# Attention, soft MoE and a squared-ReLU layer on one core: w_in converted by quarters, scores in two PSUM banks

## The chip, the cores and the metric

The kernel runs on one core of a Trainium2 chip. Times are device microseconds (us) of one execution; the kernel before took 434.12 us in the median of three runs (428.06, 434.12, 439.13). Five engines matter: PE (TensorE, matrix products into PSUM), DVE (VectorE), ACT (ScalarE), POOL (GpSimd), and the DMA queues, nearly all of whose transfers are issued by SP. Each engine takes its instructions in the order in which the program lists them; across engines they wait on semaphores.

## The reference

```python
# B=4 batches, H=8 heads, 512 local + 32 global tokens, head size 64, all float32
out_g = softmax(q_g k_all^T / 8) v_all           # 32 global tokens see all 544 keys
out_l = softmax([q_l k_g^T, band(q_l k_l^T)] / 8) [v_g, v_l]   # band: |i - j| <= 32
x = concat(out_g, out_l) -> (2176, 512)
logits = x @ phi                                 # phi (512, 32): 8 experts of 4 slots
slot_in = softmax_over_tokens(logits).T @ x      # (32, 512)
slot_out[e] = relu(slot_in[e] @ w1[e]) @ w2[e]   # w1 (8,512,1024), w2 (8,1024,512)
x = softmax_over_slots(logits) @ slot_out        # (2176, 512)
h = relu(x @ w_in)                               # w_in (512, 2048), float64 in memory
return (h * h) @ w_out                           # w_out (2048, 512), float64 in memory
```

## The kernel before, in words

Everything is written out in order by hand (no scheduler moves it), and lies in four stages.

**Attention, 0 to 169 us.** There are 44 units: 32 local ones (16 blocks of 32 queries, times two halves of the heads) and 12 global ones. Unit n goes through S (scores, `emit_S`, PE, L330 local and L336 global), mask and row minimum on DVE (L341, four instructions, from PSUM into `s_buf`), a subtraction on POOL (L354), the exponential on ACT (L364), T (four transposes on PE, L372, into the PSUM tile `pp`, copied out by ACT or DVE), and AV (products with V, L391). The loop is a software pipeline: iteration n lists S of unit n, the exponential of n-1, AV of an earlier pair, T of n-2. In between lie the transposes of new keys and queries (L219), of finished tokens (L212) and MoE logits (L442). S of a unit is 16 small products (2 head pairs, 4 batches, 2 heads e of a pair), each of which the profile records as two matmuls. A local product uses 64 of the 128 rows of the array (the half that head e owns) and 32 columns; the pair (batch, e) picks one of the four column quarters, so e=0 and e=1 never share a quarter, and all 16 write one PSUM bank, `sp`, of which there are two. A global product uses all 128 rows, with queries padded with zeros (`qgz`), and batch picks the quarter.

w_in and w_out are float64 and are turned into float32 on the chip, in blocks of 128 x 512 values (512 KB raw): `convert` is ACT abs (L540), DVE clamp and shift (L543, L546), the low word's rest (L551 on ACT or L553 on DVE), DVE join (L556), POOL add (L558). The first half of w_in, eight blocks, is converted during attention through one raw buffer `cv_raw`, at the units in the table `CONV`. The expert weights w1 and w2 are 64 pieces of 512 KB; `PIECES` says how many of them SP issues after each unit. 24 granules of SBUF ("room" a and b) can hold them at first, and more as buffers die.

**Soft MoE, 169 to 208 us.** The expert layers (`layer1` L916, `layer2` L944) use the pieces in order and free their room for the rest.

**Squared-ReLU layer, 208 to 433 us.** x @ w_in is computed as c @ G, with G = slot_out @ w_in (rank 32): `G_part`/`G_late` make G for some columns (PE, `gps`, L1023; one column quarter of the array for each 256 columns of G), `G_split` and `replicate` bring it into `G4`. There are 17 token tiles in three groups (6, 6, 5) and 16 chunks m of the 2048 hidden columns. One step (group, m) is `emit_h` (PE `hp` L1085; ACT relu L1088; DVE product L1089; then a high and low part, ACT L1095 and DVE L1096) and, one step later, `emit_o` (three 512-column matmuls per tile, L1140 to L1142, into one PSUM bank per tile). Iteration n lists h of step n, o of step n-1, then the conversion work planned for n. The order of steps is `passes`: group 0 with m 0 to 7, group 1 with m 0 to 15, group 0 with m 8 to 15, group 2 with all. At the end of a pass the tiles are copied out, or added to a saved sum (L1147, DVE). Here the remaining 8 blocks of w_in and 16 chunks of w_out are converted, one per step, over steps 0 to 23; a w_out chunk also needs `part`, ACT L859 and POOL L860, just before its first use.

Of the kernel before, what the change touches and what calls it, by code (L numbers as in the profile page):

```python
# [18 lines left out]
BIG = 3.0e38  # L19
# [5 lines left out]
def local_global_attention__soft_moe__relu2_kernel(  # L25
# [83 lines left out]
    win_sb = A.carve(NC, FF // 2)  # L109
# [6 lines left out]
    qgz = Bq.carve(HP, B, 2, QB)  # L116
# [6 lines left out]
    s_buf = Bq.carve(4, 128)  # L123
# [53 lines left out]
    def consts():  # L177
        zz = qgz.rearrange("p h b e q -> p (h b) e q")
        nc.vector.memset(zz[64:128, :, 0, :], 0.0)
        nc.vector.memset(zz[0:64, :, 1, :], 0.0)  # L180
# [49 lines left out]
    def global_q(qg_sb):  # L230
        tp = transpose4(qg_sb, ps_m, "m")
        for e in range(2):
            s = slice(64 * e, 64 * e + 64)
            evac(qgz.rearrange("p h b e q -> p (h b) e q")[s, :, e, :],
                 tp[s].rearrange("p h (b q) -> p (h b) q", b=B), e)
# [36 lines left out]
    for s in range(NJ):  # L272
# [29 lines left out]
    CONV = (4, 9, 13, 18, 22, 27, 31, 36)  # L302
    CONV_AT = (
        (0, 0, 1, 2, 3), (-1, 1, 1, 2, 3), (0, 0, 1, 2, 3), (0, 0, 0, 2, 3), (0, 1, 1, 2, 3), (0, 0, 0, 2, 3),
        (0, 1, 2, 2, 3), (0, 0, 1, 1, 2),
    )
    REST_ON_ACT = (0, 0, 1, 0, 1, 1, 1, 1)
# [5 lines left out]
        0, 0, 0, 0, 1, 2, 0, 0, 1, 1, 1, 1, 0, 1, 1, 1, 0, 0, 2, 2, 1, 0, 1, 1, 0, 1, 2, 1, 0, 1, 0, 0,  # L313
        3, 1, 0, 1, 1, 0, 1, 0, 4, 2, 2, 1,
    )

    def emit_S(n):
        kind, s, half = units[n]
        x0, s1, s2 = window(s)
        sp = ps_s.tile([128, 4, 128], F32, tag="s", name="sp")  # L320
        for h in range(2):
            hp = 2 * half + h
            for b in range(B):
                if kind == "l":
# [15 lines left out]
        for j in range(4):  # L340
            nc.vector.tensor_tensor_reduce(out=s_buf[:, j], in0=sp[:, j], in1=mk, scale=-scale, scalar=BIG,  # L341
# [12 lines left out]
        nc.gpsimd.tensor_tensor(out=pe.rearrange("p j (r k) -> p j k r", k=4), in0=s_buf.rearrange("p j (k r) -> p j k r", k=4),  # L354
# [852 lines left out]
```

## Time and profile before

| | |
|---|---|
| median of three runs | 434.12 us (428.06 to 439.13) |
| the profiled execution, whole / its span | 435.36 us / 433.5 us |
| busy share of the span: PE, DVE, ACT, POOL | 92%, 66%, 55%, 31% |
| mean granted PE clock | 0.988 of full speed |
| chain that ended last: PE, DVE, DMA, ACT | 57%, 15%, 12%, 8% |

Busy shares are means over stages with different limits; the windows and the chain of waits by stage tell more. A matmul's busy time includes its latency and overlaps its neighbours', so the pace of a run of matmuls is read from its length over its count.

### The profile page before, as it was taken

How to read it: one execution, taken by the hardware profiler on the slowest of the kernel's cores; microseconds unless marked ns; L12 is line 12 of the kernel's file. 1: busy time of each engine (PE TensorE's matmuls, PEld its weight loads, DVE VectorE, ACT ScalarE, POOL GpSimd, SP SyncE). 2: the span in 40 equal slices, each digit the busy share in tenths (PEclk: the TensorE clock that was granted, in tenths of full speed). 3: DMA queues.
4: the chain of work that ended last, by engine and by line, in shares of the span. 5: the costliest groups of instructions: out<-in, count | busy, mean ns of one | idle time of the engine just before them, and what ended most of it. 6: DMA issues, size and time to landing. Idle time of an engine off the chain costs nothing.

```text
span 433.5 us, 12427 instructions
## 1 busy us (share of the span) xinstructions
PE 400.9 (92%) x4897; PEld 306.5 (71%) x4897; DVE 287.6 (66%) x930; ACT 239.9 (55%) x561; POOL 134.4 (31%) x159
## 2 busy tenths in 40 slices
PE   6789869968889987999999999999999999999996
PEld 6677758756567764355567777777887888888884
DVE  5596947766567966310689999777997535744443
ACT  2678756878578443121656666565764534344442
POOL 6245524535346441110345532224553000000000
PEclk9999988999899999999999999999999999999999
DMA  5788894899375399899933334210000500410003
GB/s 145 193 250 220 267 279 127 284 284 305 105 222 196 88 375 356 318 409 406 406 126 98 100 103 139 97 50 0 2 0 21 121 6 0 106 42 2 0 1 121
DMA packets 54890, 69.02 MB, mean 159 GB/s; under 512 B 23856, under 2 KB 40496, under 8 KB 54832
## 3 DMA queue, kind: packets, MB, share of 16 engines
q1 hardware_dynamic: 53360, 67.19, 48.2%
q10 hardware_dynamic: 1472, 1.05, 0.8%
q8 instruction: 38, 0.62, 0.6%
q14 instruction: 20, 0.16, 0.1%
HBM read 63.77 MB, written 4.46 MB: 157 GB/s over the span
## 4 chain that ended last, share of the span: by engine, by line
PE 57%; DVE 15%; DMA 12%; ACT 8%; issue 5%; POOL 1%; SPq 1%; POOLq 0%; DVEq 0%; ACTq 0%
PE ops L1140 9%; PE ops L1141 9%; PE ops L1142 9%; PE sp L330 5%; PE xp L391 4%; PE pp L372 4%; ACT arena_b L146 4%; DVE arena_a L543 3%; DMA arena_b<-in_moe_w_in_dram 3%; DVE al L1096 3%; PE tp L219 3%; PE hps L916 2%; DMA arena_b<-in_moe_w_dram 2%; DMA arena_a<-in_moe_w_dram 2%; DVE arena_a L556 2%
## 5 line engine op out<-in xcount | busy, mean ns | idle before, releaser
L1140 PE MATMUL ops<-w_hl,ah 128*128 128x512 f32 x271 | 107.2, 395 | 0.0
L1141 PE MATMUL ops<-w_hl,ah 128*128 128x512 f32 x271 | 106.6, 393 | 0.6 <-POOL w_hl L860 0.6
L1142 PE MATMUL ops<-w_hl,al 128*128 128x512 f32 x271 | 105.7, 390 | 0.0
L1089 DVE TENSOR_TENSOR arena_a<-hp,arena_a 128x384 f32<-128x384 f32 x96 | 46.8, 529 | 45.4 <-ACT arena_a L1088 45.3
L1088 ACT ACTIVATE arena_a<-hp 128x384 f32<-128x384 f32 x96 | 40.2, 471 | 61.7 <-PE hp L1085 61.4
L1095 ACT ACTIVATE ah<-arena_a 128x384 fp32r<-128x384 f32 x96 | 45.0, 506 | 28.3 <-DVE arena_a L1089 28.3
L354 POOL TENSOR_TENSOR arena_r<-arena_b,nm 128x512 f32<-128x512 f32 x32 | 39.8, 1243 | 62.7 <-DVE nm L341 34.8
L1141 PEld LDWEIGHTS ops<-w_hl,ah 128*128 128x128 f32 x271 | 50.9, 188 | 11.6 <-POOL w_hl L860 2.8
L1142 PEld LDWEIGHTS ops<-w_hl,al 128*128 128x128 f32 x271 | 50.9, 188 | 11.1 <-DVE al L1096 0.2
L1140 PEld LDWEIGHTS ops<-w_hl,ah 128*128 128x128 f32 x271 | 50.9, 188 | 11.0 <-issue 0.8
L1096 DVE TENSOR_TENSOR al<-arena_a,ah 128x384 fp32r<-128x384 f32 x96 | 50.8, 569 | 8.9 <-ACT ah L1095 5.0
L146 ACT ACTIVATE arena_b<-tp 64x256 f32<-64x256 f32 (+2 forms) x151 | 48.8, 350 | 10.9 <-PE tp L219 5.7
L558 POOL TENSOR_TENSOR arena_a<-arena_a 128x512 int32<-128x512 int32 x23 | 29.8, 1296 | 53.1 <-DVE arena_a L556 46.2
L341 DVE CUSTOM_DVE_ANT_0 arena_b<-sp,arena_r 128x128 f32<-128x128 f32 x128 | 29.5, 286 | 20.4 <-PE sp L330 14.9
L330 PE MATMUL sp<-arena_b 64*32 64x128 f32 x1024 | 37.3, 281 | 4.0 <-issue 2.3
L330 PEld LDWEIGHTS sp<-arena_b 64*32 64x32 f32 x1024 | 27.4, 110 | 12.2 <-issue 9.7
L372 PE MATMUL pp<-ident,arena_r 128*128 128x128 f32 x176 | 29.5, 292 | 4.9 <-ACT arena_r L364 4.9
L391 PE MATMUL xp<-arena_v,arena_t 128*32 128x65 f32 x1408 | 27.2, 227 | 7.1 <-DMA arena_v<-in_v_l_dram 3.1
L364 ACT ACTIVATE arena_r<-arena_r 128x512 f32<-128x512 f32 x44 | 27.7, 629 | 9.7 <-POOL arena_r L354 9.4
L391 PEld LDWEIGHTS xp<-arena_v,arena_t 128*32 128x32 f32 x1408 | 22.7, 113 | 12.5 <-issue 6.6
L372 PEld LDWEIGHTS pp<-ident,arena_r 128*128 128x128 f32 x176 | 19.2, 144 | 12.3 <-ACT arena_r L364 6.4
L860 POOL TENSOR_TENSOR w_hl<-arena_a,w_hl 128x512 fp32r<-128x512 f32 x16 | 21.1, 1320 | 15.1 <-ACT w_hl L859 15.1
(194 smaller groups left out, 583.0 us busy)
## 6 DMA issues: line engine op xcount, KB each, us to landing
arena_a<-in_moe_w_dram SPq DMA_DIRECT2D x34, 512.0 KB, 6.1
arena_b<-in_moe_w_dram SPq DMA_DIRECT2D x23, 512.0 KB, 6.9
arena_a<-in_moe_w_out_dram SPq DMA_DIRECT2D x16, 512.0 KB, 5.3
arena_v<-in_v_l_dram SPq DMA_DIRECT2D x16, 256.0 KB, 4.4
arena_b<-in_moe_w_in_dram SPq DMA_DIRECT2D x8, 512.0 KB, 5.1
arena_a<-in_moe_w_in_dram SPq DMA_DIRECT2D x8, 512.0 KB, 3.9
arena_k<-in_k_l_dram SPq DMA_DIRECT2D x30, 128.0 KB, 4.1
arena_q<-in_q_l_dram SPq DMA_DIRECT2D x30, 128.0 KB, 3.6
```

Source lines behind the costliest of these rows:

```text
L146: nc.scalar.activation(out=out, in_=in_, func=AF.Copy)
L330: nc.tensor.matmul(sp[r + 32 * e:r + 32 * e + 32, j], qz[d, (s + 2) % 3, hp, b], keys, start=True, stop=True, tile_position=(64 * e, r + 3 ...
L354: nc.gpsimd.tensor_tensor(out=pe.rearrange("p j (r k) -> p j k r", k=4), in0=s_buf.rearrange("p j (k r) -> p j k r", k=4), in1=nm.unsqueez ...
L372: nc.tensor.transpose(pp[:, j], pe_buf[n % NPE][:, j], ident)
L391: nc.tensor.matmul(xp[32 * b:32 * b + 32, 2 * h + e], p, V[:, b, 4 * half + 2 * h + e], start=True, stop=True)
L1088: nc.scalar.activation(out=r[:, :N], in_=hp[:, :N], func=AF.Relu)
L1089: nc.vector.tensor_tensor(out=a[:, :N], in0=hp[:, :N], in1=r[:, :N], op=ALU.mult)
L1095: nc.scalar.activation(out=ah[:, s], in_=a, func=AF.Copy)
L1096: nc.vector.tensor_tensor(out=al[:, s], in0=a, in1=ah[:, s].bitcast(F32), op=ALU.subtract)
L1140: nc.tensor.matmul(op, ah[:, s], w_hi, start=begin, stop=False)
L1141: nc.tensor.matmul(op, ah[:, s], w_lo, start=False, stop=False)
L1142: nc.tensor.matmul(op, al[:, s], w_hi, start=False, stop=end)
```

## The change

1. **Quarters of w_in.** `CONV` has four blocks instead of eight; `win_sb` is half as large. Two more granules are free for weight pieces (13 in room a, 5 in a new room c, 8 in b), and `PIECES` issues some pieces earlier.
2. **Two groups take turns.** `passes` becomes group 0 with m 0 to 3, group 1 with 0 to 7, group 0 with 4 to 11, group 1 with 8 to 15, group 0 with 12 to 15, group 2 with all. 28 blocks are converted in this stage, over steps 0 to 27; their rest is always on ACT. G is made in four quarters; `G_late` runs three times, two steps before its first use, after the first tile of the step.
3. **Scores.** Each unit's scores go to two PSUM tiles, one per head e of a pair, out of three that go round; batch picks the column quarter and e the row half, for global units too (`qg` without padding). `s_buf` is doubled. To make room, `pp` has one PSUM buffer instead of two.

```diff
-    win_sb = A.carve(NC, FF // 2)
+    CW = 512
+    win_sb = A.carve(NC, CW)
...
+    s_buf = [Bq.carve(4, 128)]
...
-    room = {"a": A.granules(7, 23), "b": Bq.granules(10, 18), "t": []}
+    room = {"e": [], "a": A.granules(10, 23), "b": Bq.granules(10, 18), "c": A.granules(5, 10), "t": []}
...
-    ps_s = ps_att.enter_context(tc.tile_pool(name="ps_s", bufs=2, space=PSUM))
-    ps_pt = ps_att.enter_context(tc.tile_pool(name="ps_pt", bufs=2, space=PSUM))
+    ps_s = ps_att.enter_context(tc.tile_pool(name="ps_s", bufs=1, space=PSUM))
+    ps_pt = ps_att.enter_context(tc.tile_pool(name="ps_pt", bufs=1, space=PSUM))
...
-    CONV = (4, 9, 13, 18, 22, 27, 31, 36)
+    CONV = (4, 9, 13, 18)
...
-        0, 0, 0, 0, 1, 2, 0, 0, 1, 1, 1, 1, 0, 1, 1, 1, 0, 0, 2, 2, 1, 0, 1, 1, 0, 1, 2, 1, 0, 1, 0, 0,
+        0, 0, 0, 0, 1, 2, 0, 0, 1, 1, 1, 1, 0, 1, 1, 1, 0, 0, 2, 2, 1, 1, 1, 1, 0, 2, 2, 1, 0, 1, 1, 0,
...
+        q = qg if kind == "g" else qz[:, (s + 2) % 3]
+        sp = [ps_s.tile([128, 2, 128], F32, tag=f"s{(2 * n + e) % 3}", name=f"sp{e}") for e in range(2)]
...
+                for e in range(2):
+                    d = slice(64 * e, 64 * e + 64)
+                    k0 = kT[d, hp, b, x0]
...
+                    nc.tensor.matmul(sp[e][32 * b:32 * b + 32, h], q[d, hp, b], keys, start=True, stop=True,
+                                     tile_position=(64 * e, 32 * b))
...
-        for j in range(4):
-            nc.vector.tensor_tensor_reduce(out=s_buf[:, j], in0=sp[:, j], in1=mk, scale=-scale, scalar=BIG,
+        sb = s_buf[n % 2]
+        for j in (0, 2, 1, 3):
+            nc.vector.tensor_tensor_reduce(out=sb[:, j], in0=sp[j % 2][:, j // 2], in1=mk, scale=-scale, scalar=BIG,
...
-        seq = [("o", m) for m in range(8)] + [("i", k) for k in range(2 * NC)] + [("o", m) for m in range(8, NFC)]
+        seq = []
+        for f in range(NFC // 4):
+            if f:
+                seq += [("i", NC * f + c) for c in range(NC)]
+            seq += [("o", m) for m in range(4 * f, 4 * f + 4)]
...
+        def G_part(f, gp, c0, c1):
+            for c in range(c0, c1):
+                for j in range(2):
+                    r = 64 * (f % 2) + 32 * j
+                    nc.tensor.matmul(gp[r:r + 32], slot_outT[:, c], w_block(f, c)[:, 256 * j:256 * j + 256],
                                      start=(c == 0), stop=(c == NC - 1))
...
-        passes = [(0, 0, 8), (1, 0, 16), (0, 8, 16), (2, 0, 16)]
+        passes = [(0, 0, 4), (1, 0, 8), (0, 4, 12), (1, 8, 16), (0, 12, 16), (2, 0, 16)]
...
-        late_at = {11: (0, 2), 15: (2, 4)}
+        late_at = {first_of[4 * f] - 2: f for f in range(1, 4)}
...
-                if t == 2 and n in late_at:
-                    G_late(*late_at[n])
+                if t == 1 and n in late_at:
+                    G_late(late_at[n])
...
-                    if split and m == NFC - 1:
+                    if gi < 2 and (gi, 0, m + 1) not in passes:
                         nc.vector.tensor_tensor(out=o, in0=op, in1=o, op=ALU.add)
...
-                put_convert(n + 2, n % 2 == 1 or n == 16)
+                put_convert(n + 2, n, True)
```

Three places show how instructions move. The first is PE, a local unit late in attention, in the kernel before (L330 is S, L391 AV of a pair, L372 T, L517 an MoE product, L212 a transpose of tokens):

```order
L330 MATMUL sp<-arena_b 32x128 x16
L372 MATMUL pp<-ident,arena_r 128x128 x4
L212 MATMUL tp<-ident,arena_a 128x128 x4
L517 MATMUL msp<-arena_a,slots 32x512 x4
L330 MATMUL sp<-arena_b 32x128 x16
L391 MATMUL xp<-arena_v,arena_t 32x65 x32
```

and a like place in the changed kernel, at the end of one unit's S and the start of the next one's (L324 is S, L377 AV, L362 T, L218 a transpose of queries):

```order
L324 MATMUL sp_679<-arena_b 32x128
L324 MATMUL sp_680<-arena_b 32x128
L377 MATMUL xp<-arena_v,arena_t 32x65 x32
L362 MATMUL pp<-ident,arena_r 128x128 x4
L218 MATMUL tp<-arena_b,arena_q 128x128 x4
L324 MATMUL sp_768<-arena_b 32x128
L324 MATMUL sp_769<-arena_b 32x128
```

The 16 products now alternate between two PSUM tiles, eight times over; their number and what stands between two units are as before.

The second is SP, in the middle of attention, before (L533 loads a block of w_in, L596 expert pieces, L161 keys and queries, L173 V):

```order
L596 DMA arena_a<-in_moe_w_dram 128x1024
L533 DMA arena_b<-in_moe_w_in_dram 128x1024
L173 DMA arena_v<-in_v_l_dram 32x32x64
L161 DMA arena_k<-in_k_l_dram 32x8x128 x4
L596 DMA arena_a<-in_moe_w_dram 128x1024
L596 DMA arena_b<-in_moe_w_dram 128x1024
```

and there in the changed kernel (L576 expert pieces, L163 keys and queries, L175 V):

```order
L163 DMA arena_q<-in_q_l_dram 32x8x128 x4
L576 DMA arena_a<-in_moe_w_dram 128x1024 x2
L175 DMA arena_v<-in_v_l_dram 32x32x64
L163 DMA arena_k<-in_k_l_dram 32x8x128 x4
L576 DMA arena_a<-in_moe_w_dram 128x1024 x2
```

The load of w_in has gone, and an expert piece of the same size stands in its place.

The third is DVE at the end of a pass that falls among the conversions; before, step 7 (L1089 and L1096 belong to h, L144 copies tiles out, L543 to L556 convert):

```order
L1089 TENSOR_TENSOR arena_a<-hp,arena_a 128x384 x2
L1096 TENSOR_TENSOR al_3656<-arena_a,ah_3653 128x384 x2
L144 COPY arena_a<-ops 128x512 x3
L543 TENSOR_SCALAR arena_a<-arena_a 128x512
L546 TENSOR_SCALAR arena_a<-arena_a 128x512
L556 SCALAR_TENSOR_TENSOR arena_a<-arena_a 128x512
```

and step 19 of the changed kernel (L1084 and L1091 belong to h, L1142 adds to a saved sum, L529 to L542 convert):

```order
L1084 TENSOR_TENSOR arena_a<-hp,arena_a 128x384 x2
L1091 TENSOR_TENSOR al_3677<-arena_a,ah_3674 128x384 x2
L1142 TENSOR_TENSOR arena_a<-ops,arena_a 128x512 x6
L529 TENSOR_SCALAR arena_a<-arena_a 128x512
L532 TENSOR_SCALAR arena_a<-arena_a 128x512
L542 SCALAR_TENSOR_TENSOR arena_a<-arena_a 128x512
```

Where three copies stood on DVE (the other three on ACT), six additions stand, all on DVE, and ahead of a conversion.

## Rows read from the trace of the kernel before

**Rows 1.** Windows by stage: us, busy by engine (count), PEclk, DMA share, GB/s.
```profile
13.00:63.00 50.00, 42.62 (x1024) 34.38 (x1024) 36.74 (x189) 34.46 (x91) 23.01 (x20) 0.98 0.86 245
63.00:120.00 57.00, 50.48 (x1235) 39.12 (x1234) 37.27 (x197) 42.33 (x113) 24.77 (x23) 0.93 0.71 219
120.00:169.00 49.00, 42.65 (x1092) 32.55 (x1096) 35.58 (x184) 30.21 (x72) 22.31 (x28) 1.00 0.71 237
173.50:207.00 33.50, 32.85 (x403) 15.66 (x407) 6.36 (x23) 5.79 (x12) 3.29 (x12) 1.00 0.97 378
213.00:330.00 117.00, 115.23 (x536) 89.29 (x529) 105.02 (x188) 73.72 (x151) 49.33 (x39) 1.00 0.24 79
```
**Rows 2.** Chain of waits, shares by line, windows 13:63, 63:120 and 120:169.
```profile
by line: ACT arena_b L146 14.6%; PE sp L330 12.8%; DVE arena_b L341 10.8%; DMA arena_b<-in_moe_w_in_dram 10.4%; POOL arena_r L354 6.9%; DVE arena_b L144 5.8%; issue 5.6%; PE xp L391 4.8%; PE tp L212 4.8%; PE tp L219 4.7%; PE pp L372 4.7%; A
by line: PE sp L330 12.6%; DMA arena_b<-in_moe_w_in_dram 11.8%; ACT arena_b L146 11.6%; PE xp L391 10.8%; PE pp L372 10.5%; issue 7.6%; PE tp L219 6.3%; SPq L161 5.6%; PE sp L336 5.5%; PE msp L517 4.8%; PE lp L442 3.7%; PE tp L212 3.3%; ACT
by line: PE xp L391 17.8%; PE sp L330 17.3%; PE pp L372 16.9%; PE sp L336 8.7%; PE lp L442 7.0%; issue 6.6%; PE tp L212 4.8%; PE tp L219 3.4%; PE msp L517 3.3%; ACT arena_t L146 3.2%; ACT arena_r L364 2.3%; DVE arena_b L341 1.8%; PE tpg L42
```
**Rows 3.** Timeline of PE: start, us, line, operation, count [idle before, releaser].
```profile
78.84 1.13 PE L391 MATMUL xp<-arena_v,arena_t 128*32 128x65 f32 x64
86.20 1.08 PE L330 MATMUL sp<-arena_b 64*32 64x128 f32 x32
212.56 1.07 PE L1023 MATMUL gps<-arena_a,slots 128*32 128x256 f32 x16
291.72 1.92 PE L1023 MATMUL gps<-arena_a,slots 128*32 128x256 f32 x16
```
**Rows 4.** Waits in 13:169, all engines: us in total, times, longest us.
```profile
ACT arena_b L540 <- DMA arena_b<-in_moe_w_in_dram: 10.3, 4, 4.5
DVE arena_b L341 <- POOL arena_r L354: 7.4, 8, 1.3
```
**Rows 5.** Timeline, two successive T of units and the first one's copy.
```profile
85.62 0.65 PE L372 MATMUL pp<-ident,arena_r 128*128 128x128 f32 x4
87.70 0.60 PE L372 MATMUL pp<-ident,arena_r 128*128 128x128 f32 x4
88.23 0.60 ACT L146 ACTIVATE arena_t<-pp 128x512 f32<-128x512 f32 x1
```
**Rows 6.** Timeline, S of a unit and the first minimum of the unit before.
```profile
82.97 1.08 PE L330 MATMUL sp<-arena_b 64*32 64x128 f32 x32
83.02 0.28 DVE L341 CUSTOM_DVE_ANT_0 arena_b<-sp,arena_r 128x128 f32<-128x128 f32 x1
```
**Rows 7.** Timeline of PE at the end of the soft MoE.
```profile
206.62 1.91 PE L944 MATMUL ops<-arena_b,c_all 128*32 128x256 f32 x26 [0.65 <-DMA arena_b<-in_moe_w_dram]
```
**Rows 8.** Timeline of PE, last stage: a step with G_late, a plain step.
```profile
268.88 0.51 PE L1085 MATMUL hp<-cstack,G 128*128 128x384 f32 x2
271.22 1.92 PE L1023 MATMUL gps<-arena_a,slots 128*32 128x256 f32 x16 [0.45 <-DVE arena_a L1089]
275.94 0.51 PE L1085 MATMUL hp<-cstack,G 128*128 128x384 f32 x2
339.20 0.51 PE L1085 MATMUL hp<-cstack,G 128*128 128x384 f32 x2
343.65 0.51 PE L1085 MATMUL hp<-cstack,G 128*128 128x384 f32 x2
```
**Rows 9.** Timeline of POOL and DVE, the clamp of a conversion in step 7.
```profile
250.16 1.29 POOL L860 TENSOR_TENSOR w_hl<-arena_a,w_hl 128x512 fp32r<-128x512 f32 x1 [0.74 <-ACT w_hl L859]
250.23 1.51 DVE L543 TENSOR_SCALAR arena_a<-arena_a 128x512 f32<-128x512 f32 x1
```
**Rows 10.** Groups of instructions, tiles kept apart by shape: busy us, mean ns.
```profile
L1096 DVE TENSOR_TENSOR al<-arena_a,ah 128x384 fp32r<-128x384 f32 x80 | 45.4, 600 | 8.9 <-ACT ah L1095 5.0
L1089 DVE TENSOR_TENSOR arena_a<-hp,arena_a 128x384 f32<-128x384 f32 x80 | 41.5, 552 | 45.4 <-ACT arena_a L1088 45.3
L1147 DVE TENSOR_TENSOR arena_a<-ops,arena_a 128x512 f32<-128x512 f32 x6 | 3.7, 682 | 0.0
```

More of the change, by code (lines that the diff above doesn't have):

```diff
@@ L122, in local_global_attention__soft_moe__relu2_kernel @@
     perm = Bq.carve(128)
-    s_buf = Bq.carve(4, 128)
+    s_buf.append(Bq.carve(4, 128))
     assert Bq.used <= 10 * GR
@@ L231, in global_q @@
         tp = transpose4(qg_sb, ps_m, "m")
[L232 to L235, printed above, removed]
+        for n in range(2):
+            h = slice(2 * n, 2 * n + 2)
+            evac(qg[:, h], tp[:, h].rearrange("p h (b q) -> p h b q", b=B), n)
     def item_k(i, half, who=1):
@@ L353, in emit_S @@
             nm = new
-        nc.gpsimd.tensor_tensor(out=pe.rearrange("p j (r k) -> p j k r", k=4), in0=s_buf.rearrange("p j (k r) -> p j k r", k=4),
+        nc.gpsimd.tensor_tensor(out=pe.rearrange("p j (r k) -> p j k r", k=4), in0=sb.rearrange("p j (k r) -> p j k r", k=4),
                                 in1=nm.unsqueeze(2).unsqueeze(3).to_broadcast([128, 4, 4, QB]), op=ALU.subtract)
@@ L589, in load_piece @@
             return raw_load()
-        at = next((r for r in ("tba" if kind == 2 and e >= 4 else "tab") if room[r]), None)
+        at = next((r for r in ("tcba" if kind == 2 and e >= 4 else "tcab") if room[r]), None)
         if at is None:
@@ L669, in local_global_attention__soft_moe__relu2_kernel @@
                     at(l1, pos, fn, i, d=d + dd)
-        for n in range(NC * WRES):
+        for n in range(NC):
             split, clamp, shift, rest, join = win_convert(n)
@@ L681, in local_global_attention__soft_moe__relu2_kernel @@
         after(("l", NJ - 2, 1), give, "b", 7, 8)
-        after(("l", 11, 1), give, "at", 6, 7, d=av_at(index["l", 11, 1]) - index["l", 11, 1] + MOE_D[2])
+        after(("l", 11, 1), give, "at", 4, 5, d=av_at(index["l", 11, 1]) - index["l", 11, 1] + MOE_D[2])
         after(("g", NJ - 1, 1), free, "b", 2, 6)
@@ L829, in raw_load @@
             q = len(raws)
-            if q == len(seq) or not room["a"]:
-                return False
-            raws[q] = g = room["a"].pop(0)
+            at = next((r for r in "ae" if room[r]), None)
+            if q == len(seq) or at is None:
+                return False
+            g = room[at].pop(0)
+            raws[q] = g, at
             kind, k = seq[q]
@@ L984, in local_global_attention__soft_moe__relu2_kernel @@
         assert nxt[0] == len(order)
-        yro = [room["a"].pop(0) for _ in range(3)]
-        win2 = [room["a"].pop(0) for _ in range(NC)]
-        while raw_load():
-            pass
-        put_convert(0, True, True)
-        put_convert(1, True)
+        yro = [room["a"].pop(0) for _ in range(2)]
+        room["e"] = A.granules(5, 8)
+        raw_load()
         def now(*names):
@@ L996, in local_global_attention__soft_moe__relu2_kernel, with w_block @@
         layer2(1, 2, 6)
+        yro.append(room["a"].pop(0))
+        win2 = [room["a"].pop(0) for _ in range(4)]
+        def w_block(f, c):
+            if f == 0:
+                return win_sb[:, c]
+            return win2[2 * (f % 2) + c // 2][:, CW * (c % 2):CW * (c % 2) + CW]
+        put_convert(0, 0, True, True)
+        put_convert(1, 0, True)
         now(("split", 0))
         layer2(1, 6, 8)
+        while raw_load():
+            pass
         now(("mask", 0), ("rest", 0))
@@ L1143, in emit_o @@
                 if end:
[L1144 to L1146 removed]
+                    op = o_t.pop((gi, t))
+                    o = saved[gi][t] if gi < 2 else o_buf[t % 5]
+                    if gi < 2 and (gi, 0, m + 1) not in passes:
                         nc.vector.tensor_tensor(out=o, in0=op, in1=o, op=ALU.add)
```

104 lines of the change are left out of this document (35 added, 69 removed).

## The prediction, written before the changed kernel ran

> **What bounds the kernel now.** I read the windows by stage first. In attention PE is the busiest engine: 42.6 of 50 us, 50.5 of 57 and 42.7 of 49, with ACT and DVE at 34 to 42 [rows 1]. Then the chain of waits for the same three windows. From 63 us on it runs mostly through PE; in the first 50 us ACT, DVE and POOL hold more of it than PE does [rows 2]. Scores (L330, L336) are 12.8% of the first window, 18.1% of the second, 26.0% of the third: 6.4 + 10.3 + 12.7 = 29.4 us in which the chain stands on scores. In the expert layers the DMA engines are 0.97 busy, and the chain ends in weight transfers there, but PE is busy for 32.85 of 33.5 us [rows 1], and the last wait for a weight is 0.65 us [rows 7]: the two are balanced, and freeing the one alone gains under 1 us. In the last stage a plain step takes 343.65 - 339.20 = 4.45 us of PE [rows 8]. From 213 to 330, while conversions run, PE has 115 of 117 us and DVE 105 [rows 1]: PE ends last, but DVE has a tenth to spare at most.
>
> **Scores.** The trace shows what sets their pace. A G_part over four column quarters runs 16 records in 1.07 us, a G_late over two quarters needs 1.92 us for 16 records of the same shape [rows 3]: the pace goes with the number of tiles of the array at work. The 32 records of a unit's S take 1.08 us [rows 3] with four tiles at work, the last one's latency in it; I take the advance as about 1.02. The change puts eight tiles to work (four quarters, two row halves). No row here has two row halves in one quarter. One bound is 1.02, unchanged; the other comes from AV, whose records are shorter and are paced by issue: 64 in 1.13 us [rows 3], 17.7 ns each, so 32 x 17.7 ns = 0.57 us. Half of 1.02 is 0.51, below that. I take 0.57, because a tile's speed depended on nothing but its own queue in the two G rows. That is 44% less, or 13.0 of the 29.4 us.
>
> [...]
>
> Not all of the 13.0 us comes off the end. In the first window the other engines hold the chain, so I count half of 6.4 x 0.44 = 2.8, that is 1.4. For the other two I count four fifths of 23.0 x 0.44 = 10.1, that is 8.1, since ACT (42.3 of 57) and DVE (35.6 of 49) come next and a run of in-order engines does not close up fully. **-9.5 us** (0 to -13.0).
>
> **Four conversions leave attention.** ACT waited 10.3 us in 4 places for raw blocks of w_in [rows 4], and ACT's queue behind it holds the copies and exponentials that PE needs. Two of the four waits belong to blocks that go, so 0 to 5 us. But SP lists an expert piece where the load stood, so V and keys still queue behind 512 KB. **-2 us.** The four blocks' ACT, DVE and POOL work beside it lies off the path: nothing.
>
> **Doubled `s_buf`.** DVE waited 7.4 us in 8 places until POOL had read the one buffer [rows 4]. DVE's minima hold 10.8% of the chain in the first window and under 2% in the third [rows 2]: **-1 us** (0 to -5).
>
> **What the banks cost.** With one `pp`, T of a unit must wait for the copy of the T before it. At 85.62 and 87.70 two T run, and the first one's copy begins at 88.23 and ends at 88.83 [rows 5]: T would have waited 1.1 us. I find 8 such places among 44, 4.8 us in all at today's pace, and PE stands on the path there. Where the copy was late behind a conversion that goes, the wait goes too; a faster PE makes others. **+3.5 us** (0 to +8). With three score tiles in turn, the second product of S of unit n+1 waits until DVE has taken the first two minima of unit n. S at 82.97 began before the first minimum at 83.02 [rows 6]; there are 7 such places, the widest 0.6 us: **+1.5** (0 to +4).
>
> Attention: -9.5 - 2 - 1 + 3.5 + 1.5 = **-7.5 us**.
>
> **Soft MoE.** Two more granules and 3 more pieces issued before attention ends bring the last pieces about 3 us earlier relative to PE, but PE's wait there is 0.65 us [rows 7]: **-0.5**.
>
> **The last stage.** The rest on ACT takes DVE work away; everything else adds.
> - *PE.* A third G_late costs 1.92 us [rows 8], the first quarter's G_part two quarters in 1.92 instead of four in 2 x 1.07: **+1.7**.
> - *Wait in G_late.* Its PSUM tile `gps` shares two buffers with `hp`, so it starts only when DVE has made the step's first product (L1089). Before, it came after two tiles and still waited 0.45 us [rows 8]; after one tile it asks 0.65 us earlier. The product stands behind the conversion of the step before on DVE. Conversions with a `part` end late: the clamp takes 1.51 us when POOL's L860 runs beside it [rows 9]. I take 1.1 us for each of three, less 0.45: **+3** (0.5 to 7).
> - *Additions.* The pass that ends at step 19 puts 6 x 0.68 = 4.1 us [rows 10] on DVE ahead of a conversion, where three copies (about 2 us) stood. The step holds product and low part, 4 x at most 0.60 = 2.4, plus a conversion of about 1.5, so 8 us against PE's 4.45; one step of slack, since the low part is wanted one step later, absorbs about half. **+2** (0 to 4). At steps 27 and 31 no conversion follows: nothing. The earlier passes end with three copies on DVE as before, twice among the conversions in either kernel.
> - *DVE's slack.* Chunks of w_out now come in fours, with four w_in blocks (no `part`) between, and no rest is on DVE. So the 1.1 us that a clamp loses beside POOL (1.51 us, most of it while POOL still runs) [rows 9] falls on four steps in a row at most, not on eight, and DVE catches up in between. Of the 2 us that PE had idle between 213 and 330 [rows 1] I give back **-1.2** (0 to -2).
>
> Sum +5.5. SP's raw loads stay 9 deep at the start and 6 later, one per step of 4.45 us: hidden while DMA is 0.24 busy [rows 1]. POOL's work moves with DVE's and never ended last here.
>
> **Sum.** 435.4 - 7.5 - 0.5 + 5.5 = 432.9 for the profiled execution, which stood 1.2 us above the median of the runs; against that median, about **431 to 432 us**. I say 431.
>
> **The rivals.**
> 1. *Attention closes up fully.* Scores give 12 to 13 us, evacuations catch up and the one `pp` costs 1, while the last stage pays 4. Time: 434.1 - 12.5 - 3 + 2.5 + 4 - 0.5, about 424 or a little less. For it: PE is 85 to 89% busy in all three windows. Against it: ACT and DVE are over two thirds busy in the first. It would come in at 418 to 425.
> 2. *Two row halves in one quarter take turns.* Then S stays at 1.02 or worse. If unchanged, the banks' waits stand alone: 434.1 - 3 + 5 - 0.5 + 5.5, about **441**; if switching halves costs a little on top, S at 1.2 instead of 1.02, 44 x 0.18 x about 0.7 of it on the path adds 5.5 us: 447, slower. It decides from about 1.1 us per unit up. For it: no row shows the case. Against it: the two G rows. [...]
> 3. *DVE bounds the last stage.* If its conversions fall one step behind for good (10% spare is little, and three more passes' ends press on it), each of the 28 blocks costs 0.3 us more and each G_late 2.5: +5.5 + 5.5 + 4 = +15. With attention at -7.5: about 441. It decides where DVE's step exceeds 4.45 in the w_in steps too; that PE was idle for under 2 of 117 us there before [rows 1] speaks against it.
> 4. *Scores do not reach the path.* The one `pp` and the three-way turn hold PE as long as S did: attention 0, last stage +5.5: 439.
>
> **Chances.** The forecast (424 to 437 of its own) 0.52, rival 1 0.20, rival 2 0.10, rival 3 0.08, rival 4 0.10. About 2% (8.7 us, so below 425.4 or above 442.8) is what can be told from no change here. Below 425.4 lie most of rival 1 and a tail of the forecast: 0.25. Above 442.8 lie half of rivals 2 and 3 and little else: 0.12. The rest, 0.63, is within. The range that leaves out 2 in 10 is 419 to 443.
>
> **What would show it.** S: the 32 records of a unit in 0.55 to 0.65 us instead of 1.08; above 1.0 rival 2 holds. Attention: the last AV about 7 us earlier than before; PE idle before T with the copy of `pp` as releaser, some 3 to 4 us in all, more in rival 4. Last stage: plain steps at 4.45, three steps with `gps` near 7.5, one of about 6.5 after step 19; and PE's first `hp` to its last 5 to 6 us longer. If that stretch is as long as before, the additions and G_late were hidden and the sum is too high by 5; if attention is longer, the banks were mis-sized and the prediction is wrong in its main term.

## The result, and the profile after

The changed kernel takes 436.94 us (median of 5 runs, 434.26 to 440.69), 1.0143 times the kernel before (95% interval 1.0096 to 1.0191): about 6.2 us slower, where 431 was forecast, 2 to 3 us faster. In what follows 1% is 4.3 us. Every ratio compares the fast executions (within 1.5% of the fastest of their kernel) with those of the kernel before in the same batch of runs, so it is not the quotient of two medians. Between two kernels that are compared through their ratios, the interval is about 0.7%, 3 us, either way. Its profiled execution took 436.94 us, with a span of 435.1.

The windows by stage, columns as in [rows 1]:
```profile
13.00:63.00 50.00, 40.37 (x1033) 30.14 (x1040) 36.74 (x190) 35.51 (x96) 22.46 (x20) 0.86 0.79 227
63.00:120.00 57.00, 46.92 (x1243) 34.56 (x1237) 36.39 (x196) 41.00 (x113) 22.68 (x22) 0.91 0.76 236
120.00:169.00 49.00, 41.03 (x1107) 29.25 (x1109) 34.62 (x186) 27.22 (x67) 19.44 (x27) 0.97 0.72 233
173.50:207.00 33.50, 33.50 (x461) 17.68 (x457) 6.42 (x22) 8.60 (x17) 4.83 (x15) 1.00 0.95 366
213.00:330.00 117.00, 111.45 (x508) 86.65 (x507) 104.79 (x184) 75.55 (x154) 44.41 (x35) 1.00 0.27 87
```
PE has less to do in attention (128.3 us in the three windows, 135.8 before), yet does about the same number of instructions in the same time: it idles 27.7 us instead of 20.2. Its granted clock is lower too, 0.86 and 0.91 in the first two.

The last stage took about as long as forecast. On PE's timeline the first `hp` starts at 207.95 and the last at 423.93: 215.98 us, against 212.04 to 422.26, 210.22 us, before. The steps with G_late and the one after the additions (line L1080 starts a step):
```profile
240.13 0.51 PE L1080 MATMUL hp<-cstack,G 128*128 128x384 f32 x2
242.54 1.92 PE L1019 MATMUL gps<-arena_a,slots 128*32 128x256 f32 x16 [1.20 <-DVE arena_a L1084]
248.59 0.51 PE L1080 MATMUL hp<-cstack,G 128*128 128x384 f32 x2
282.94 1.92 PE L1019 MATMUL gps<-arena_a,slots 128*32 128x256 f32 x16 [1.23 <-DVE arena_a L1084]
311.97 0.51 PE L1080 MATMUL hp<-cstack,G 128*128 128x384 f32 x2
317.37 0.91 PE L1080 MATMUL hp<-cstack,G 128*128 128x384 f32 x2 [0.54 <-DVE arena_a L1084]
322.57 0.51 PE L1080 MATMUL hp<-cstack,G 128*128 128x384 f32 x2
325.21 1.92 PE L1019 MATMUL gps<-arena_a,slots 128*32 128x256 f32 x16 [1.43 <-DVE arena_a L1084]
```
`gps` waits 1.20 to 1.43 us for DVE's first product, three times; the steps around the additions take 5.40 and 5.20 us instead of 4.45.

Attention is where the forecast failed. The chain of waits by line in 63:120, against the second row of [rows 2]:
```profile
by line: DMA arena_v<-in_v_l_dram 31.8%; PE xp L377 13.2%; ACT arena_b L148 10.9%; issue 8.4%; ACT arena_t L148 7.0%; PE pp L362 6.4%; PE sp L324 5.3%; PE tp L218 4.1%; ACT arena_r L354 4.0%; DVE arena_b L331 2.4%; PE msp L503 1.9%; ACT are
```
Scores fell from 18.1% to 5.3%. Their place is taken by loads of V, absent from the leading lines of that row before. The pieces of the chain from 85 to 111 us (start, us, what):
```profile
85.54 0.60 PE sp L324 x32
...
86.72 1.06 PE xp L377 x64
...
87.85 6.78 DMA arena_v<-in_v_l_dram
...
94.68 1.16 PE xp L377 x58
...
95.91 5.73 DMA arena_v<-in_v_l_dram
...
101.68 2.01 PE xp L377 x64
...
103.71 5.63 DMA arena_v<-in_v_l_dram
...
109.38 1.21 PE xp L377 x63
```
It is a loop. V holds three blocks, so `load_v(s + 3)` is issued only after AV of block s, and the AV of block s + 1 needs it. One turn is AV, 1.1 us, and the load's landing, counted from the start of its issue by SP (L175, 0.60 us of it): in the three turns shown 5.6 to 6.8 us, so 7.0 to 8.0 us from one pair of AV to the next, whatever PE does in between. By the median landing of 4.5 us a turn would be 5.6. Such a load lies in 14 of the 21 steps from pair to pair. In 11 of the 14, AV starts less than 0.2 us after its V has landed, and nothing faster in S can shorten those turns.

PE's timeline shows S itself, and what happens to its pace:
```profile
33.40 0.65 PE L324 MATMUL sp<-arena_b 64*32 64x128 f32 x27
35.99 0.41 PE L324 MATMUL sp<-arena_b 64*32 64x128 f32 x5 [1.94 <-issue]
37.86 1.11 PE L324 MATMUL sp<-arena_b 64*32 64x128 f32 x32
38.90 1.71 PE L377 MATMUL xp<-arena_v,arena_t 128*32 128x65 f32 x64
41.56 0.67 PE L324 MATMUL sp<-arena_b 64*32 64x128 f32 x32
```
At 41.56, where the granted clock was 1.00, 32 records of S take 0.67 us with the last one's latency, and 0.60 in the chain above, where the next instruction follows. At 37.86 they take 1.11. The windows around it (columns as in [rows 1]):
```profile
33.00:36.00 3.00, 1.06 (x34) 0.62 (x32) 0.00 (x0) 2.81 (x10) 0.96 (x1) 1.00 0.83 242
36.00:39.00 3.00, 3.00 (x49) 2.09 (x52) 2.14 (x10) 1.04 (x4) 1.36 (x2) 0.63 0.53 148
```
After PE had stood still for 1.94 us, the granted clock in 36:39 was 0.63, and in its last two us, 37:39, it was 0.50.

### The profile page after: what moved, and what is told of

Same layout as the page of the kernel before. It is cut to its first block, busy times and chain, and to the rows that moved or that the text cites. A ratio compares the mean times of both kernels' runs of the same rounds, so it can differ in the third digit from the quotient of the medians.

```text
span 435.1 us, 12444 instructions
## 1 busy us (share of the span) xinstructions
PE 391.2 (90%) x4897; PEld 292.5 (67%) x4897; DVE 294.6 (68%) x932; ACT 243.9 (56%) x571; POOL 133.1 (31%) x159
## 3 DMA queue, kind: packets, MB, share of 16 engines
q10 hardware_dynamic: 1472, 1.05, 0.8%
## 4 chain that ended last, share of the span: by engine, by line
PE 52%; DVE 19%; DMA 11%; ACT 10%; issue 6%; SPq 1%; POOL 1%; ACTq 0%; DVEq 0%
PE ops L1135 9%; PE ops L1136 8%; PE ops L1137 8%; DMA arena_v<-in_v_l_dram 8%; PE xp L377 4%; DVE al L1091 4%; ACT arena_b L148 4%; PE hps L903 3%; DVE arena_a L529 3%; PE ops L931 3%; PE sp L324 3%; DVE arena_a L1084 2%; PE tp L218 2%; PE pp L362 2%; DVE arena_a L532 2%
## 5 line engine op out<-in xcount | busy, mean ns | idle before, releaser
L1084 DVE TENSOR_TENSOR arena_a<-hp,arena_a 128x384 f32<-128x384 f32 x96 | 46.7, 528 | 37.5 <-ACT arena_a L1083 37.5
L1135 PEld LDWEIGHTS ops<-w_hl,ah 128*128 128x128 f32 x271 | 50.9, 188 | 11.7 <-issue 1.5
L1137 PEld LDWEIGHTS ops<-w_hl,al 128*128 128x128 f32 x271 | 50.9, 188 | 11.5 <-DVE al L1091 0.6
L1091 DVE TENSOR_TENSOR al<-arena_a,ah 128x384 fp32r<-128x384 f32 x96 | 52.4, 585 | 8.9 <-ACT ah L1090 5.0
L544 POOL TENSOR_TENSOR arena_a<-arena_a 128x512 int32<-128x512 int32 x27 | 34.9, 1294 | 66.9 <-DVE arena_a L542 64.4
L377 PE MATMUL xp<-arena_v,arena_t 128*32 128x65 f32 x1408 | 29.1, 234 | 15.6 <-DMA arena_v<-in_v_l_dram 8.1
L324 PE MATMUL sp<-arena_b 64*32 64x128 f32 x1408 | 34.9, 298 | 4.5 <-ACT arena_b L148 2.1
L377 PEld LDWEIGHTS xp<-arena_v,arena_t 128*32 128x32 f32 x1408 | 24.0, 118 | 22.0 <-DMA arena_v<-in_v_l_dram 11.1
L362 PE MATMUL pp<-ident,arena_r 128*128 128x128 f32 x176 | 31.3, 305 | 4.6 <-ACT arena_t L148 4.2
L324 PEld LDWEIGHTS sp<-arena_b 64*32 64x32 f32 x1408 | 20.5, 115 | 16.1 <-issue 9.7
L148 ACT ACTIVATE arena_t<-pp 128x512 f32<-128x512 f32 x32 | 19.1, 598 | 17.0 <-PE pp L362 16.7
L362 PEld LDWEIGHTS pp<-ident,arena_r 128*128 128x128 f32 x176 | 20.4, 151 | 12.0 <-issue 6.3
```

The lines of the kernel that those rows point to most:

```text
L148: nc.scalar.activation(out=out, in_=in_, func=AF.Copy)
L324: nc.tensor.matmul(sp[e][32 * b:32 * b + 32, h], q[d, hp, b], keys, start=True, stop=True, tile_position=(64 * e, 32 * b))
L362: nc.tensor.transpose(pp[:, j], pe_buf[n % NPE][:, j], ident)
L377: nc.tensor.matmul(xp[32 * b:32 * b + 32, 2 * h + e], p, V[:, b, 4 * half + 2 * h + e], start=True, stop=True)
L1084: nc.vector.tensor_tensor(out=a[:, :N], in0=hp[:, :N], in1=r[:, :N], op=ALU.mult)
L1091: nc.vector.tensor_tensor(out=al[:, s], in0=a, in1=ah[:, s].bitcast(F32), op=ALU.subtract)
```

## The experiments

The theory after the traces was that **V's loop** bounds attention now. The rivals: the **banks** (one `pp`, three score tiles) hold PE; PE's **instruction blocks** come too slowly; the **clock** falls when PE idles and takes back what S gave.

### One part of the change at a time

`e1_scores_only`: the kernel before with the new `emit_S`, `emit_AV`, `global_q`, banks and two `s_buf`; w_in in halves.

> The kernel before with the new scores alone (even and odd heads in two banks, one pp, two s_buf); w_in and the last stage as before. V-load theory (after faster scores attention is held by the loop AV, load of the next V block, AV): S takes 0.60 us per unit, PE waits for arena_v in six or more places of 2 to 6 us, the first hp comes within 4 us of before's 212.0 and the time is 0 to 1% below before. Bank theory (one pp and the score tiles hold PE): the same time, but the waits stand before T and before S, not before AV. If the scores had reached the path as I forecast, 6 us or more below before (-1.5%). The last stage, first hp to last, stays at 210 us in all of them.

Measured: 438.30 us, ratio 1.0129 (1.0080 to 1.0178). The new scores with their banks cost 5.6 us by themselves; the last stage is 210.2 us, as before. Both theories had it 0 to 1% faster than before; it is slower. PE's waits in 13:169 point to neither alone: 5.1 us for V in five places, not six or more of 2 to 6 us each, and 11.7 us put to "issue", a wait for nothing that the profile shows.

`e2_quarters_only`: the changed kernel with the old `emit_S`, `emit_AV`, `global_q` and banks.

> The changed kernel with the scores as before (four tiles, two pp, one s_buf); only the quarters of w_in and the turns of the two token groups are left of the change. If the last stage is worth what its steps show (first hp to last 216.0 against 210.2), this is slower than before by 5.8 us less what four conversions give back in attention (0 to 3 us): +0.7 to +1.4%. If the last stage's cost were an effect of attention's end (pieces and raw blocks that land later), the stretch would be near 210 and the time within 0.5% of before.

Measured: 434.77 us, 1.0048 (0.9997 to 1.0098), last stage 216.0 us. So the quarters cost 5.8 there and give 3.7 back ahead of it (2.1 - 5.8; the interval allows 1.6 to 5.9). Forecast was -2 for the conversions and -0.5 for the soft MoE, which lies within that.

`e4_two_pp`: the banks taken away again, from the changed kernel.
```
-ps_pt ... bufs=1                          +ps_pt ... bufs=2
-sp = [ps_s.tile([128, 2, 128], ..., tag=f"s{(2*n+e) % 3}") for e in range(2)]
+if n == 0:
+    s_all[:] = [ps_s.tile([128, 2, 2, 128], ..., tag=f"s{e}") for e in range(2)]
+sp = [s_all[e][:, n % 2] for e in range(2)]
```


> The changed kernel with two pp again: the scores of even heads lie in the two halves of one bank in turn, those of odd heads in another, which frees the third. V-load theory: within 0.5% of the changed kernel (437), the waits for arena_v as long as there. Bank theory: 3 to 6 us below it (431 to 434), since no T waits for the copy of the T before and S waits for no minimum. If a bank that DVE reads while PE writes its other half costs something, minima or S get longer and it is slower than the changed kernel.

Measured: 433.82 us, 1.0053 (1.0001 to 1.0106). The banks cost 3.9 us (about 1 to 7), near the 3.5 + 1.5 of the forecast. But without them the new scores stand level with the old ones of `e2_quarters_only`: 0.2 us apart, about 3 either way.

### V

`e3_no_v`, `e13_old_no_v` and `e14_two_pp_no_v` leave out the loads of V from the fourth block on (13 of the 16 loads; the first expectation counts 12 of 15), in the changed kernel, in `e2_quarters_only` and in `e4_two_pp`. The later units then multiply old values of V:
```
-for s in range(NJ - 2): late.setdefault(av_at(last_of(s)), []).insert(0, (load_v, (s + 3,)))
+late.setdefault(av_at(last_of(0)), []).insert(0, (load_v, (3,)))
```


> The changed kernel without the loads of V after the third block (12 of 15 blocks; the later windows then multiply old values, so the output is not the reference's). V-load theory: the waits of PE for arena_v (6 us and more between 63 and 165) go, attention ends 5 to 9 us earlier, about 428 to 432 us (1 to 2% below the changed kernel); expert pieces come a little sooner too. Bank theory: the waits move to T and S and attention ends less than 2 us earlier, 435 to 437.

> The quarters with the scores as before (e2_quarters_only) without the loads of V after the third block (the output is not the reference's). V-load theory: the old scores fill the time that a V load takes, so little goes: within 2 us of e2_quarters_only (434.8), 433 to 435. If V held the old scores as much as the new ones: 4 us and more below it.

> The kernel with two pp (e4_two_pp) without the loads of V after the third block. V-load theory: 5 to 9 us below e4_two_pp (433.8) and 4 us or more below e13_old_no_v: without V the new scores win. Fetch and clock theory: within 2 us of e13_old_no_v, since what PE gains it loses to its own instruction blocks and to the half clock in either kernel.

Measured: `e3_no_v` 433.78 us, 1.0005 (0.9956 to 1.0054), 6.0 us below the changed kernel. The other two, 430.71 and 426.65 us, complete a square of ratios to the kernel before:

| | V loaded | V left out |
|---|---|---|
| old scores, two `pp` | 1.0048 | 0.9943 (0.9899 to 0.9988) |
| new scores, two `pp` | 1.0053 | 0.9853 (0.9785 to 0.9921) |

The loads hold the new scores by 2.0% (8.6 us), the old ones by 1.05% (4.5 us). Without V the new scores win 0.9%, 3.9 us (the intervals leave 0.4 to 7). So V's loads take about 4 us of what S gives; but this is a difference of two differences, its interval is about 5 us either way, and it is not clear of nothing. That the loads held the old scores as well was not expected. Two things are not told apart here: the loop, and the 3.4 MB less on the DMA queues.

A second trace of the kernel before shows that V holds the old scores, too.

> The kernel before once more, for a second trace of it. Instruction-fetch theory (PE's own instructions, read in blocks of 128 matmuls with their weight loads, arrive too slowly where faster scores use them up sooner): PE's idle time put to issue in 13:169 stays at 3 to 7 us, against 9 to 12 us in the two kernels with faster scores (e1_scores_only, e4_two_pp). Clock theory: the granted clock is 0.97 or more on average there. If issue is as long here as in those two, the fetch is no cause.

Measured: 432.20 us. Its chain in 63:120:
```profile
by line: PE xp L391 14.3%; PE sp L330 12.4%; PE pp L372 12.0%; DMA arena_v<-in_v_l_dram 11.4%; PE tp L219 8.4%; DMA arena_b<-in_moe_w_in_dram 8.3%; SPq L161 6.3%; PE sp L336 5.9%; POOL arena_r L354 5.3%; PE tp L212 3.7%; PE msp L517 3.5%; A
```
V has 11.4% here and no leading place in [rows 2]: the loop was within reach of PE's own pace, and one trace's leading lines can miss it. Turn by turn, neither trace does: in either, AV starts less than 0.15 us after its V has landed in 5 of the 14 turns.

Two attempts on the loop failed. `e6_v_first` (from `e4_two_pp`) moves the expert pieces of the step ahead of a V load behind it.

> The kernel with two pp (e4_two_pp) with the expert pieces of the step ahead of a V load issued behind it instead, so that V stands behind 512 KB pieces no longer. V-load theory: the median landing of V falls from 4.5 us to 3.5 or less, PE's waits for arena_v (7.9 us in five places) fall under 4, and the time by 2 to 4 us. Clock theory: less, 1 to 2 us, where the idle time falls under what lets the clock drop. If V was only the last of several waits: nothing, and the releaser before AV becomes another.

Measured: 437.35 us, 1.0145 (1.0081 to 1.0210), 4 us slower; V lands in 5.0 us by the median, not 3.5, and PE waits 11.1 us for it, not under 4. To move these pieces behind V is no help.

`e10_no_pieces` (from `e4_two_pp`) sets the first 16 entries of `PIECES` to 0. The two after them are 0 as it is, so no piece is issued in the first 18 units, not 28 as the expectation says: the first one is issued at 68.4 us.

> The kernel with two pp (e4_two_pp) without expert pieces in the first 28 of 44 units; they are all issued later, so the experts come late, and only the stretch up to unit 28 is to be compared. If V loads and PE's instruction blocks are late because 512 KB pieces share the DMA engines with them: V lands in 3 us or less there, waits for arena_v and issue stalls vanish, and unit 28 is reached 6 us or more earlier than in e4_two_pp. If the landing of V is set by its own 1024 rows of 256 bytes: V still takes 4 us and most waits stay.

The DMA issues in 13:60, of `e10_no_pieces`:
```profile
arena_v<-in_v_l_dram SPq DMA_DIRECT2D x6, 256.0 KB, 4.4
```
and of `e4_two_pp`:
```profile
arena_v<-in_v_l_dram SPq DMA_DIRECT2D x6, 256.0 KB, 4.9
```
Both medians have the first two loads in them, which take about 5 us in either kernel. The five behind them take 3.4 to 4.9 us without pieces (median 3.7), and 3.4 to 6.4 with them (median 4.6): the pieces cost V something, but most of the landing is its own, or that of keys, queries and w_in beside it. The exponential of the 18th unit starts 49.1 us after that of the first, against 52.5; but it is 49.8 in `e12_new_scores_g4`, with the attention of `e4_two_pp` and all pieces, so one trace does not tell these apart.

`e15_v_batches` and `e16_old_v_batches` (from `e12_new_scores_g4` and `e11_old_scores_g4`, below) load V as two pairs of batches and take AV of a pair of units in that order.
```
-for h in range(2): for e in range(2): for b in range(B): matmul(xp[32*b:32*b+32, ...
+for b0 in (0, 2): for m, xp in pair: for h ...: for e ...: for b in (b0, b0 + 1): matmul(xp[32*b:...
```


> The new scores with two pp and the last stage of e12_new_scores_g4 (428.0), with V loaded as two pairs of batches and the 64 records of a pair of AV taken in that order, so that the load of the first pair is issued after half of AV and AV goes on when it has landed. The loop AV, load, AV is 0.57 us shorter in some ten places. V-load theory: 2 to 5 us below e12_new_scores_g4. If the second DMA's issue (0.6 us) and its own landing eat that: the same time.

> The same with the scores as before (against e11_old_scores_g4, 428.6). V-load theory: less than with the new scores, 0 to 2 us, since PE has more of its own to do between two AV.

Measured: 431.59 us, 0.9970 (0.9930 to 1.0011), and 432.02, 1.0010 (0.9974 to 1.0046): 0.9% and 1.2% slower than their bases. The timeline of `e15_v_batches` says why:
```profile
84.40 1.84 PE L387 MATMUL xp<-arena_v,arena_t 128*32 128x65 f32 x64
92.17 1.84 PE L387 MATMUL xp<-arena_v,arena_t 128*32 128x65 f32 x64 [2.29 <-DMA arena_v<-in_v_l_dram]
```
A batch is a column quarter, so either half of AV had two quarters to work on, and 64 records took 1.84 us instead of 1.13 [rows 3]: 20 times 0.7 us more. PE's waits for V did fall, from 9.7 to 4.5 us with the new scores and from 5.5 to 2.8 with the old. The edit changed two things, and does not tell what the shorter loop is worth.

### Instruction blocks

`e8_scores_twice` (from `e4_two_pp`): `for h in (0, 1, 0, 1)` in `emit_S`.

> The kernel with two pp (e4_two_pp) in which the 32 records of every unit's scores are done twice, the second time over the first: 44 x 0.6 = 26 us more PE work, and every score 0.6 us later. If the scores are on the path, 10 us and more slower than e4_two_pp. Clock theory: the clock in 13:169 comes back to 0.97 or more, as in the kernel with the old scores, and the time stays within 1% of e4_two_pp.

Measured: 460.59 us, 1.0672 (1.0617 to 1.0727), about 27 us slower than `e4_two_pp` and than `e2_quarters_only`. The granted clock in the three windows was 0.90, 0.94 and 0.93, not the 0.97 that the clock theory asked for. It is not the length of S alone: a doubled S takes 1.16 us on PE's timeline, and the old S of `e2_quarters_only` 1.08, which makes 3.5 us for 44 units. PE's timeline shows what else:
```profile
90.49 0.77 PE L381 MATMUL xp<-arena_v,arena_t 128*32 128x65 f32 x37 [2.48 <-issue]
101.27 1.37 PE L328 MATMUL sp<-arena_b 64*32 64x128 f32 x63 [1.83 <-issue]
114.55 0.77 PE L381 MATMUL xp<-arena_v,arena_t 128*32 128x65 f32 x37 [1.28 <-issue]
125.03 0.55 PE L381 MATMUL xp<-arena_v,arena_t 128*32 128x65 f32 x22 [3.14 <-issue]
```
Such stalls sum to 22.7 us in 13:169:
```profile
PE xp L381 <- issue: 15.8, 8, 3.6
PE sp L328 <- issue: 6.9, 6, 1.8
```
From the first of the four to the second PE did 254 matmuls by the timeline, then 378, then 263: close to two, three and two times 128 (some records are missing or counted twice). The page's instruction queue, before, and in `e4_two_pp` just the same:
```profile
q8 instruction: 38, 0.62, 0.6%
```
and in `e8_scores_twice`:
```profile
q8 instruction: 49, 0.80, 0.7%
```
11 packets more for 44 x 32 = 1,408 matmuls more: one per 128 matmuls and their weight loads, of 16 KB each (0.80 MB in 49). So PE's program is fetched in blocks. The traces also hold the time of each packet: in the eleven traces that are compared here and in the next lines, all 78 of these stalls in 13:169 end 1.2 to 1.6 us after a packet of this queue has landed. So a PE that has used up a block waits for the next. Summed over 13:169, PE's issue stalls are 6.5 and 5.3 us in the two traces of before, 2.5 in `e2_quarters_only`, 4.7 in `e11_old_scores_g4`; with the new scores 6.2 in the changed kernel, 9.1 in `e4_two_pp`, 11.7 in `e1_scores_only`, 7.3 in `e12_new_scores_g4`. That is some 4 us more on average, though not in every pair; without V they are alike, 10.6 and 11.3, and in `e15_v_batches` and `e16_old_v_batches` both are small, 2.5 and 2.1. Part of what S gives goes there when V is loaded; no run takes these stalls away by themselves.

### The clock

`e5_filler` (from `e4_two_pp`): four products of `ident` by itself into `xp` ahead of each pair of AV.

> The kernel with two pp (e4_two_pp) and, ahead of each pair of AV, four products of the identity by itself into the tile that AV overwrites: 20 times about 0.9 us of PE work that nobody needs, done where PE mostly waits. Clock theory (the idle time that faster scores leave makes the chip grant half the clock, and PE then loses there what it had gained): the granted clock in 13:169 rises from about 0.92 to 0.97 or more, and the time falls by 2 to 5 us against e4_two_pp in spite of the added work. If the clock costs nothing on the path: unchanged to 5 us slower. V-load theory alone: unchanged, since PE waits for V there anyhow.

Measured: 440.73 us, 1.0221 (1.0168 to 1.0274), about 7 us slower than `e4_two_pp`. The granted clock in 13:63 and 63:120 was 0.97, against 0.90 and 0.91; but it was 0.97 and 0.94 in `e12_new_scores_g4`, too, whose attention is that of `e4_two_pp` without any filler. So two traces do not show that the filler raised it. What the rows do show is what PE did before it fell: in the traces of the changed kernel, `e4_two_pp` and `e5_filler`, PE had stood still for 1.5 to 3.2 us at a time shortly ahead of each fall up to 169 us. What the clock costs by itself stays open.

The V-load theory missed as well: it had the time unchanged, since PE waits for V there anyhow. PE's waits for V did fall from 7.9 to 1.1 us, and all its idle time between the first AV and the last from 23.4 to 12.3; but that is 11 of the 18 us of added work (20 times 0.9), and the rest came on top.

### The last stage, and a better version

`e7_late3`: the changed kernel with `t == 3` for `G_late` and `t == 5` for the replicate behind it.

> The changed kernel with G_late after three tiles of its step instead of after one, the replicate that follows after five. As I priced it, the wait of gps for the step's first product (1.20, 1.23 and 1.43 us) goes to under 0.3 in each of three steps: the last stage is 3 to 4 us shorter than 216.0, and the time 3 to 4 us below the changed kernel, if nothing later waits for the replicated rows. If DVE is late in those steps by more than two tiles, the wait only shrinks and under 2 us come back.

Measured: 435.05 us, 1.0048 (1.0003 to 1.0093), 0.95% or 4 us below the changed kernel. The last stage is 212.98 us, 3.0 shorter, and `gps` waits for nothing:
```profile
242.05 1.92 PE L1019 MATMUL gps<-arena_a,slots 128*32 128x256 f32 x16
```
`e11_old_scores_g4` and `e12_new_scores_g4` (from `e2_quarters_only` and `e4_two_pp`) add to this a G of four column quarters:
```
-for j in range(2): r = 64*(f%2) + 32*j
-    matmul(gp[r:r+32], slot_outT[:, c], w_block(f, c)[:, 256*j:256*j+256], ...)
+for j in range(4):
+    matmul(gp[32*j:32*j+32, :128], slot_outT[:, c], w_block(f, c)[:, 128*j:128*j+128], ...)
```
with a `sel` of 64 rows in `replicate`, one for either half of the columns.

> The quarters with the scores as before (e2_quarters_only), G_late after three tiles, and G of a quarter of w_in computed as four column groups of 128 columns instead of two of 256 (about 0.98 us instead of 1.92, by the 64 records of gd in 1.96 us), the replicate as two pairs of 128 columns. Last stage: 216.0 - 3.0 (e7_late3) - 3 x 0.94 - about 1 for the first part = 209 to 211 us, with up to 1 us more for the replicates. The time 5 to 6 us below e2_quarters_only, so about 0.5 to 1% below the kernel before.

> The same last stage with the new scores and two pp (e4_two_pp). If the new scores give nothing even with two pp, the time of e11_old_scores_g4 within 0.5%; if fetch stalls and the half clock eat more than they give, 1 to 3 us above it; if they give what I forecast, 5 us and more below it.

Measured: 428.62 us, 0.9886 (0.9812 to 0.9960), and 428.02, 0.9879 (0.9807 to 0.9950). Both beat the kernel before, by 5 us, with a last stage of 211.3 us. A step of `e12_new_scores_g4` with G_late takes 6.6 us instead of 8.5:
```profile
235.97 0.51 PE L1086 MATMUL hp<-cstack,G 128*128 128x384 f32 x2
238.46 1.21 PE L1024 MATMUL gps<-arena_a,slots 128*32 128x128 f32 x32
241.19 0.66 PE L1043 MATMUL rps<-ghl,sel 64*128 64x128 f32 x4
242.58 0.51 PE L1086 MATMUL hp<-cstack,G 128*128 128x384 f32 x2
```
The two are level, to about 4 us either way: the new scores add nothing with V loaded, as in the square.

## Why the prediction was wrong

- **Scores, pace: right.** 0.57 us forecast, 0.60 measured. That issue paces AV, behind the 0.57, was the author's estimate; what the runs show is that 64 AV records take 1.84 us on two quarters (`e15_v_batches`), not 1.13. Rival 2 is out: with two row halves at work in each quarter, S took 0.60 us instead of 1.01, so the halves work side by side.
- **Scores, -9.5 us on the path: the step that failed.** It took half of what S gives in the first window and four fifths in the other two off the end, because ACT and DVE come next. Measured: 0.2 us slower with two `pp`, about 3 either way, which is the edge of its own range (0 to -13.0). Without V 3.9 of the 9.5 us come, so about 4 us are V's, by the square, and 5.6 do not come even then.
- **V's loop could have been seen** in the trace of before, though not by medians: AV 1.13 [rows 3] and a landing of 4.4 make 5.5 us a turn, against 6.5 us for two units (139.3 us from the first exponential to the 44th), and two units of S give 0.8. But single landings took 3.4 to 7.1 us, and in 5 of the 14 turns AV starts less than 0.15 us after the landing: work that PE did ahead of it, such as an S of 1.08 us, only filled the time of the landing. If every turn gives back its own slack, and no more than 0.8 us, 6.8 of 11.5 us are left. This estimate puts the loop at about 5 us, near the 4 of the square.
- **Banks, +5: right within the noise** (3.9). Rival 4 named them alone for a gain of nothing and gave 439; it was nearest in time, but without the banks the scores still gave nothing.
- **Conversions and soft MoE, -2.5:** -3.7, with -2.5 inside its interval. **The doubled `s_buf`** was not measured alone.
- **Last stage, +5.5: right** (+5.8 in the trace): three waits of 1.20 to 1.43 us for 1.1, and 1.7 us around the additions for 2.

Measured: 0.2 (scores) + 3.9 (banks) - 3.7 + 5.8 = +6.2 us. These are differences along one row of kernels, so they must add up; the sum is no check. The range held the time; the direction was wrong.

Where did the gain of S go? The windows from the first AV to the last, columns as in [rows 1], for the two kernels with old scores (`e2_quarters_only`, `e11_old_scores_g4`) and the two with new scores and two `pp` (`e4_two_pp`, `e12_new_scores_g4`):
```profile
23.40:156.60 133.20, 119.14 (x3120) 94.47 (x3116) 94.43 (x512) 93.41 (x241) 58.72 (x55) 0.99 0.77 235
23.20:160.30 137.10, 121.24 (x3120) 96.45 (x3116) 93.46 (x505) 93.25 (x240) 58.90 (x55) 0.96 0.75 229
22.80:160.50 137.70, 114.35 (x3125) 84.09 (x3116) 94.21 (x504) 92.95 (x240) 59.10 (x55) 0.93 0.74 228
23.10:156.90 133.80, 108.17 (x3123) 80.05 (x3116) 93.19 (x504) 92.72 (x240) 58.79 (x55) 0.97 0.76 235
```
What the lower clock can cost is at most the length times one less PEclk: 1.3 and 5.5 us with the old scores, 9.6 and 4.0 with the new. PE's busy time less that is 116.8 us on average with the old scores and 104.5 with the new, so S gives about 12 us here. PE's idle time grows by 9.5 us on average: 4.8 put to issue (the instruction blocks), 3.0 to V and 1.8 to ACT. The clock takes up to 3.4. That is all of the 12. It is an estimate from two traces of either kind, and it tells where the time stood, not what each cause is worth by itself: with V gone, part of it moved to the others. That remains open.

## What to carry to other kernels

Before an engine's work is made shorter, look for loops that hold no engine: a ring's last use, the load's issue, its landing and the next use, summed and set against the period, turn by turn and not by medians. Price such a loop even when the trace shows it waiting once: an AV that starts just as its load has landed waits for it, too. And a wait taken for the price of a change (`gps` behind one tile) is often a matter of two places in the order.

## What the runs showed of the hardware

- 32 score records took 0.60 us on eight tiles of the array and 1.01 on four (chain of waits, the changed kernel and before); 64 AV records 1.13 us on four quarters and 1.84 on two (before and `e15_v_batches`). Half the tiles at work made it 1.6 to 1.7 times as long.
- PE's instructions came in packets of 16 KB, one per 128 matmuls with their weight loads (11 more for 1,408 more matmuls), and stalls for them of up to 3.6 us were seen (`e8_scores_twice`). All 78 in eleven traces ended 1.2 to 1.6 us after a packet had landed.
- A load of V, 256 KB in 1,024 rows of 256 bytes, landed 3.4 to 7.1 us after its issue began, 4.4 by the median (before).
- After PE had stood still for 1.94 us the granted clock was 0.63 in 36:39 and 0.50 in 37:39 (the changed kernel); after 3.07 us of it, up to 93.00, it was 1.00 in 93:96 (before).
